# Decode attention with a feed-forward branch: keys one item ahead of values, the feed-forward input product as moving rows in mid-stream, output weights used earlier

## The chip, the cores and the metric

The kernel runs on one core of one Trainium2 chip. The metric is the time of one execution on the device in microseconds (us), as the median of several runs. The core has a matrix engine (TensorE, PE in the profile; its loads of the stationary operand are PEld), a vector engine (VectorE, DVE), an activation engine (ScalarE, ACT), a general engine (GpSimd, POOL) and a queue engine that issues transfers (SyncE, SP). Sixteen DMA engines move the data from memory into the core's on-chip buffer.

## The reference

One token per sequence (two sequences, `B = 2`) is decoded through two branches, and a gate mixes them:

```python
# x: (2, 1, 640); k_cache, v_cache: (2, 32, 4096, 128); wq: (640, 4096); wo: (4096, 640)
# w1: (640, 1728); w2: (1728, 640); all float32
g = sigmoid((x * gate_w).sum(-1, keepdims=True))
q = (x @ wq) split in 32 heads of 128
p = softmax(einsum("bhqd,bhkd->bhqk", q, k_cache) * 128 ** -0.5)
a = einsum("bhqk,bhkd->bhqd", p, v_cache) joined over heads @ wo
b = silu(x @ w1) @ w2
out = g * a + (1 - g) * b
```

Nearly all bytes are the two caches: 2 x 32 heads x 4096 positions x 128 numbers, once for keys and once for values, 268 MB together. Every byte is used once.

## The kernel before, in words

**Items.** The work is cut into 32 items, one for each pair of heads and sequence (`items`, L57). An item has one slab of keys and one of values, each 128 partitions x 8192 numbers (4 MB). Partition p holds 64 consecutive positions of one of the two heads.

**What is done with an item.** `mul` multiplies the keys in place by the query, which stands in every partition: columns from 44 of 64 on in GpSimd (L271), the others in two pieces on VectorE (L275). `scores` sums over the head dimension on VectorE (L281) and takes a maximum per partition (L284). `peak` turns these maxima on TensorE (`mt`, L288) and VectorE takes the maximum of each head (`mx`, L290). `weights` spreads it (`mb`, L296, `nb`, L298) and takes the exponentials on ScalarE (`pz`, L301). `total` adds the sums (`tot`, L312). `values` multiplies the weights with the values on TensorE, 16 products of 512 columns that go in turn to four groups of 32 output partitions (`pv`, L325). `combine` copies (`osb`, L336) and adds these groups (`po`, L339). `invert` (`rinv`, L317) and `scale` (`oT`, L348) divide, apply the gate and store the item's column for the output product.

**The loop.** In iteration i of the loop at L385 the program issues, in this order: the first piece of `mul` of item i, `peak` and `weights` of item i-1, the second piece of `mul` and `scores` of item i, and then `total`, `values`, `combine`, `invert` and `scale` of item i-1. Each engine takes its instructions in the order in which they are written (`manual_schedule`, L53).

**Slabs and the stream.** All large transfers go through five slabs (`SLOTS = 5`, L43). The list `stream` (L62 to L71) gives their order: query weights `wq` (first of three parts), input weights `w1`, then keys and values of each item in turn, the other parts of `wq` and the first part of the output weights `wo` after items 7, 13 and 18, and at the end `wo` part 1, `w2` and `wo` part 2. `pump` (L102) issues them on SP in this order; the transfer at place m of the list takes the slab of the one at place m-5 and so waits, on SP, until that one has been used up (`spend`). SP waits at the head of its queue, so a transfer that waits holds back all behind it. The last 64 rows of `w2` have a small tile of their own (`w2t`, L406).

**Before the loop.** `gates` makes the gate, `query_rows(0, ...)` (L237) multiplies x with the first part of `wq`, with x as the stationary operand and the weights as moving rows, `query(0)` (L253) spreads the query of the first head pair, and `ffn_in` (L195 to L214) makes the hidden vector of the feed-forward branch: for each of 14 groups of hidden units, five products with a 128-column piece of `w1` as the stationary operand and the two columns of x as moving data (`ph`, L202), then the SiLU and the gate on ScalarE and VectorE (L209 to L213).

**Output products.** `project(grp)` (L352) rearranges the results of two head pairs (`pp`, L356), copies them (`oP`, L365) and adds their product with four rows of weights to the bank `acc` (L184). Groups 0 to 2 are done in iteration 14, groups 3 to 5 behind the loop, then `ffn_out` (hidden vector times `w2`), groups 6 and 7 and the product with `w2t`. A copy (`ot`, L413) and two transfers end the program.

Of the kernel before, what the change touches and what calls it, by code (L numbers as in the profile page):

```python
# [8 lines left out]
F32 = mybir.dt.float32  # L9
# [6 lines left out]
def tile_gated_decode(  # L16
# [42 lines left out]
    QCH = ((0, 6), (6, 12), (12, HP))  # L59
    WOG = ((0, 3), (3, 6), (6, 8))  # L60

    stream = [("wq", 0), ("w1", 0)]  # L62
    for i in range(N):
        stream += [("k", i), ("v", i)]
        if i == 7:
            stream.append(("wq", 1))
        if i == 13:
            stream.append(("wo", 0))
        if i == 18:
            stream.append(("wq", 2))  # L70
    stream += [("wo", 1), ("w2", 0), ("wo", 2)]  # L71
    T = {}
    spent = set()
    nxt = [0]
# [106 lines left out]
    def accumulate(lhsT, w):  # L181
        m = lhsT.shape[1]
        for n in range(G):
            nc.tensor.matmul(  # L184
                acc[32 * n : 32 * n + m, :],
                lhsT,
                w[:, n * W : (n + 1) * W],
                start=(done[0] == 0),
                stop=(done[0] == NMM - 1),
            )  # L190
        done[0] += 1

    def ffn_in():  # L195
        w = T["w1", 0].rearrange("p (j f) -> p j f", j=J)
        ph = ps_s.tile([P, 512], F32, tag="sm", name="ph")
        for n in range(FR + 1):
            m = P if n < FR else FT
            for j in range(J):  # L200
                cols = w[:, j, n:FM:FR] if n < FR else w[:, j, FM:F]
                nc.tensor.matmul(  # L202
                    ph[:m, n * B : (n + 1) * B], cols, xs[:, :, j], start=(j == 0), stop=(j == J - 1)
                )
        for n0, n1, m in ((0, FR, P), (FR, FR + 1, FT)):
            k = n1 - n0
            src = ph[:m, n0 * B : n1 * B].rearrange("p (n b) -> p n b", b=B)
            e = const.tile([P, k, B], F32, name=f"he{n0}")[:m]
            nc.scalar.activation(e, src, AF.Exp, scale=-1.0)  # L209
            nc.vector.tensor_scalar_add(e, e, 1.0)  # L210
# [3 lines left out]
        spend("w1", 0)  # L214

    def ffn_out():
        w = T["w2", 0]
# [124 lines left out]
    def scale(i):  # L342
        hp, b = items[i]
        grp = hp // 2
        if grp not in O:
            O[grp] = const.tile([P, 4, B], F32, name=f"oT{grp}")
        h = 2 * (hp % 2)
        nc.vector.scalar_tensor_tensor(  # L348
            O[grp][:, h : h + 2, b], PO[i][:, :2], g[:, b : b + 1], R[i], op0=ALU.mult, op1=ALU.mult
        )  # L350

    def project(grp):  # L352
        pp = ps_s.tile([P, 512], F32, tag="sm", name="pp")
        for n in range(4):
            for h in range(4):
                nc.tensor.matmul(  # L356
                    pp[32 * h : 32 * h + 32, n * B : (n + 1) * B],
                    ident[:, n : P : 4],
                    O[grp][:, h, :],
                    start=True,  # L360
                    stop=True,
                )
        first = done[0] == 0
        oP = o_first if first else work.tile([P, 4, B], F32, name="oP")
        nc.scalar.copy(oP[:, :, :B], pp[:, : 4 * B].rearrange("p (n b) -> p n b", b=B))  # L365
# [12 lines left out]
    late = {  # L380
        8: [lambda: query_rows(1, 0), lambda: query_rows(1, 1)],
        14: [lambda: project(0), lambda: project(1), lambda: project(2)],
        19: [lambda: query_rows(2, 0), lambda: query_rows(2, 1)],
    }
    for i in range(N + 1):  # L385
        if i < N:
            mul(i, 0)
        if i >= 1:
            peak(i - 1)
            weights(i - 1)  # L390
        if i < N:
            mul(i, 1)
            scores(i)
            if i + 1 < N and items[i + 1][1] == 0:
                query(items[i + 1][0])
        if i >= 1:
            total(i - 1)
# [8 lines left out]
    nc.sync.dma_start(w2t, w2[FM:, :])  # L406
# [32 lines left out]
```

## Time and profile before

| | |
|---|---|
| median of 3 runs | 721.2 us (720.84 to 721.53) |
| the profiled execution's own time | 720.26 us |
| its span, first to last instruction | 718.5 us |
| bytes moved | 298.64 MB, mean 416 GB/s |
| busy: VectorE, TensorE, GpSimd, ScalarE | 501.2, 372.0, 181.8, 63.4 us |
| mean granted clock of TensorE | 0.659 |

The profile is of one execution. Its times count from the start of the span; the execution's own time is 1.76 us longer than its span. The page cuts the span in 40 slices of 18 us and gives for each the busy tenths of every engine, the granted clock of TensorE and what the DMA engines moved. The views by stretches give the same for stretches that one chooses. The chain of waits follows the work that ended last back from the end. For a transfer the profile gives the time from its issue on SP to its landing. A product in 32-bit numbers shows as two records on TensorE, so 16 products are 32 records.

### The profile page before, as it was taken

The numbers are of one execution on the slowest core, as the hardware profiler recorded it, in microseconds if no ns is written. First come the engines' busy times: TensorE is split into PE (matmuls) and PEld (weight loads), VectorE is DVE, ScalarE is ACT, GpSimd is POOL, SyncE is SP. The second block draws the span as 40 slices with busy tenths as digits, with TensorE's granted clock in tenths as the row PEclk, the third lists the DMA queues.
The fourth block names the chain that finished last, engine by engine and source line by source line (L and its number), as shares of the span: only waits on it lengthen the run. The fifth ranks groups of instructions, "written<-read, shape, count | busy, mean of one in ns | idle before, by whom it ended". The sixth has DMA issues, their size and how long they took to land.

```text
span 718.5 us, 5865 instructions
## 1 busy us (share of the span) xinstructions
PE 372.0 (52%) x2474; PEld 189.5 (26%) x2474; DVE 501.2 (70%) x247; ACT 63.4 (9%) x225; POOL 181.8 (25%) x44
## 2 busy tenths in 40 slices
PE   3992556454508455450845543544455545443476
PEld 1792222222203122220412221221122222221135
DVE  1006999878837777883777885777778887777740
ACT  0000011010100101010010100100010101000010
POOL 1023332123332222332222233332222333333300
PEclk9755576656658655665765565756665666666679
DMA  9999599999999999999999999999999999999993
GB/s 354 432 438 409 236 409 437 427 431 426 416 442 437 427 431 429 434 417 441 431 430 431 431 421 432 430 434 424 433 434 431 432 425 433 434 431 429 422 429 153
DMA packets 13162, 298.64 MB, mean 416 GB/s; under 512 B 1672, under 2 KB 1680, under 8 KB 3664
## 3 DMA queue, kind: packets, MB, share of 16 engines
q1 hardware_dynamic: 12712, 298.26, 97.1%
q8 instruction: 19, 0.31, 0.2%
q10 hardware_dynamic: 424, 0.01, 0.0%
q14 instruction: 7, 0.06, 0.0%
HBM read 298.26 MB, written 0.01 MB: 415 GB/s over the span
## 4 chain that ended last, share of the span: by engine, by line
DMA 53%; DVE 25%; PE 19%; ACT 1%; issue 1%; SPq 0%; DVEq 0%; ACTq 0%
DMA k<-in_A_k_cache_dram 50%; DVE k L275 12%; DVE s L281 12%; PE pv L325 8%; PE ph L202 5%; DMA w<-in_B_w_dram 3%; PE acc L184 2%; PE mb L296 1%; PE q L253 1%; PE tot L312 1%; ACT pz L301 1%; PE pp L356 1%; DVE mx L290 1%; PE po L339 0%; DVE he L210 0%
## 5 line engine op out<-in xcount | busy, mean ns | idle before, releaser
L271 POOL TENSOR_TENSOR k<-k,qsb 128x2560 f32<-128x2560 f32 x32 | 179.8, 5618 | 497.4 <-DMA k<-in_A_k_cache_dram 419.5
L275 DVE TENSOR_TENSOR k<-k,q 128x3072 f32<-128x3072 f32 x64 | 196.8, 3076 | 125.5 <-DMA k<-in_A_k_cache_dram 125.5
L281 DVE TENSOR_REDUCE s<-k 128x64 f32<-128x8192 f32 x32 | 278.0, 8686 | 3.7
L325 PE MATMUL pv<-v,pz 128*32 128x512 f32 x1024 | 183.5, 881 | 0.0
L296 PE MATMUL mb<-mx,nsc 1*128 1x1 f32 x128 | 31.4, 345 | 217.8 <-DVE mx L290 217.8
L296 PEld LDWEIGHTS mb<-mx,nsc 1*128 1x128 f32 x128 | 28.7, 309 | 230.1 <-DVE mx L290 224.8
L325 PEld LDWEIGHTS pv<-v,pz 128*32 128x32 f32 x1024 | 40.4, 153 | 113.1 <-issue 112.6
L288 PE MATMUL mt<-ident,m 128*1 128x128 f32 x64 | 15.0, 325 | 65.3 <-DVE m L284 65.3
L339 PE MATMUL po<-sel,osb 128*128 128x2 f32 x256 | 33.7, 254 | 22.9 <-ACT osb L336 22.9
L339 PEld LDWEIGHTS po<-sel,osb 128*128 128x128 f32 x256 | 31.0, 191 | 53.4 <-ACT osb L336 53.4
L298 ACT COPY nb<-mb 128x1 f32<-128x1 f32 x32 | 5.1, 160 | 359.5 <-PE mb L296 359.5
L336 ACT COPY osb<-pv 128x512 f32<-128x512 f32 x32 | 18.8, 586 | 196.5 <-PE pv L325 196.5
L202 PE MATMUL ph<-xs,w 128*128 128x2 f32 (+1 forms) x140 | 34.6, 385 | 1.3 <-DMA w<-in_B_w_dram 1.3
L202 PEld LDWEIGHTS ph<-xs,w 128*128 128x128 f32 (+1 forms) x140 | 34.5, 347 | 1.5 <-DMA w<-in_B_w_dram 1.5
L210 DVE TENSOR_SCALAR he<-he 128x26 f32<-128x26 f32 (+1 forms) x2 | 1.3, 636 | 47.7 <-ACT he L209 47.7
L312 PE MATMUL tot<-rs,ones 128*128 128x2 f32 x64 | 18.4, 357 | 21.1 <-ACT pz L301 20.9
L312 PEld LDWEIGHTS tot<-rs,ones 128*128 128x128 f32 x64 | 15.6, 304 | 26.8 <-ACT pz L301 26.8
L301 ACT ACTIVATE pz<-s,nb 64x64 f32<-64x64 f32 x64 | 22.1, 345 | 1.4
L288 PEld LDWEIGHTS mt<-ident,m 128*1 128x1 f32 x64 | 3.0, 81 | 68.7 <-DVE m L284 49.3
L237 PE MATMUL qr<-wq,xz 128*32 128x512 f32 (+1 forms) x100 | 19.4, 543 | 3.3 <-DMA wq<-in_A_wq_dram 3.3
L253 PE MATMUL q<-qrow,spread 64*128 64x128 f32 x64 | 18.0, 428 | 0.0
L348 DVE SCALAR_TENSOR_TENSOR oT<-po,g,rinv 128x2 f32<-128x2 f32 x32 | 7.0, 219 | 9.9 <-PE po L339 6.7
(49 smaller groups left out, 112.5 us busy)
## 6 DMA issues: line engine op xcount, KB each, us to landing
k<-in_A_k_cache_dram SPq DMA_DIRECT2D x32, 4096.0 KB, 27.2
v<-in_A_v_cache_dram SPq DMA_DIRECT2D x32, 4096.0 KB, 33.4
wo<-in_A_wo_dram SPq DMA_DIRECT2D x8, 1280.0 KB, 22.9
wq<-in_A_wq_dram SPq DMA_DIRECT2D x2, 3840.0 KB, 27.1
w<-in_B_w_dram SPq DMA_DIRECT2D x1, 4320.0 KB, 22.4
w<-in_B_w_dram SPq DMA_DIRECT2D x1, 4160.0 KB, 32.7
wq<-in_A_wq_dram SPq DMA_DIRECT2D x1, 2560.0 KB, 22.7
w2t<-in_B_w_dram SPq DMA_DIRECT2D x1, 160.0 KB, 22.1
```

Of the source, the lines that this page charges most:

```text
L202: nc.tensor.matmul(ph[:m, n * B : (n + 1) * B], cols, xs[:, :, j], start=(j == 0), stop=(j == J - 1))
L237: nc.tensor.matmul(ps[32 * hh : 32 * hh + 32, : (e - s) * DH], xz[:, j, :], w[:, j, s:e, hh, :], start=(j == 0), stop=(j == J - 1),)
L253: nc.tensor.matmul(qps[hp][:, b, :], spread[:, b, :], qrow[n][:, c : c + DH], start=True, stop=True)
L271: nc.gpsimd.tensor_mul(k[:, CV:, :], k[:, CV:, :], qsb[hp][:, b, None, :].to_broadcast([P, C - CV, DH]))
L275: nc.vector.tensor_mul(k[:, c0:c1, :], k[:, c0:c1, :], qps[hp][:, b, None, :].to_broadcast([P, c1 - c0, DH]))
L281: nc.vector.reduce_sum(S[i], kview(i), axis=AX.X)
L296: nc.tensor.matmul(mb[:, :1], nsc[:, hh, :], M[i][:, hh : hh + 1], start=(hh == 0), stop=(hh == 1))
L301: nc.scalar.activation(pz[i % NPZ][lo:hi, :, 4 * hh : 4 * hh + 4], S[i][lo:hi].rearrange("p (g c) -> p g c", c=4), AF.Exp, bias=nb[lo:hi], ...
L312: nc.tensor.matmul(t[:, :2], ones, rs2[i % NPZ], start=True, stop=True)
L325: nc.tensor.matmul(PV[i][32 * q : 32 * q + 32, :], pz[i % NPZ][:, gr, :], v[:, gr, :], start=(gr < 4), stop=(gr >= NG - 4),)
L336: nc.scalar.copy(osb.rearrange("p c d -> p (c d)"), PV[i])
L339: nc.tensor.matmul(po[:, :2], osb[:, c, :], sel[:, c : 8 : 4], start=(c == 0), stop=(c == 3))
```

## The change

- **Order of the stream.** Behind `wq` comes the first key slab. From there the keys of item i+1 stand ahead of the values of item i. `w1` stands behind the values of item 2, the other parts of `wq` and the first part of `wo` behind those of items 8, 12 and 19, and `wo` part 1 behind those of item 25. The end of the list is `w2` and `wo` part 2.
- **Feed-forward input product.** `ffn_in` now takes x (padded to 32 columns, `xz`) as the stationary operand and `w1` as moving rows: 4 column quarters of 416 into four groups of 32 output partitions, five products each, and five of 64 columns for the rest. ScalarE copies the rows (`hrow`), and 53 small products against the identity turn them into the same `ph` as before. It is called in iteration 3, and its SiLU (`ffn_act`) in iteration 4.
- **Output products.** `project` is split in `permute` (`pp`, `oP`) and the product itself. Groups 0 to 2 are done in iteration 13, groups 3 to 5 in iteration 26. Behind the loop both remaining groups are permuted first, then come `ffn_out` and the two products. `oP` has three buffers.
- `query(0)` now comes between the two parts of `query_rows(0, ...)`.

The core of the diff:

```diff
+    extra = {2: ("w1", 0), 8: ("wq", 1), 12: ("wo", 0), 19: ("wq", 2), 25: ("wo", 1)}
-    stream = [("wq", 0), ("w1", 0)]
+    stream = [("wq", 0), ("k", 0)]
     for i in range(N):
-        stream += [("k", i), ("v", i)]
...
-    stream += [("wo", 1), ("w2", 0), ("wo", 2)]
+        if i + 1 < N:
+            stream.append(("k", i + 1))
+        stream.append(("v", i))
+        if i in extra:
+            stream.append(extra[i])
+    stream += [("w2", 0), ("wo", 2)]
...
+    QF = FM // 4
+
     def ffn_in():
         w = T["w1", 0].rearrange("p (j f) -> p j f", j=J)
+        rows = ps_s.tile([P, 512], F32, tag="sm", name="hr")
+        for j in range(J):
+            for c in range(4):
+                nc.tensor.matmul(
+                    rows[32 * c : 32 * c + 32, :QF],
+                    xz[:, j, :],
+                    w[:, j, c * QF : (c + 1) * QF],
+                    start=(j == 0),
+                    stop=(j == J - 1),
+                )
+        hrow = const.tile([P, QF + FT], F32, name="hrow")
+        nc.scalar.copy(hrow[:, :QF], rows[:, :QF])
+        tail = ps_s.tile([P, 512], F32, tag="sm", name="hr")
+        for j in range(J):
+            nc.tensor.matmul(
+                tail[:32, :FT], xz[:, j, :], w[:, j, FM:F], start=(j == 0), stop=(j == J - 1)
+            )
+        nc.scalar.copy(hrow[:32, QF:], tail[:32, :FT])
+        spend("w1", 0)
         ph = ps_s.tile([P, 512], F32, tag="sm", name="ph")
-        for n in range(FR + 1):
-            m = P if n < FR else FT
-            for j in range(J):
-                cols = w[:, j, n:FM:FR] if n < FR else w[:, j, FM:F]
+        for n in range(FR):
+            for c in range(4):
+                q = slice(32 * c, 32 * c + 32)
                 nc.tensor.matmul(
-                    ph[:m, n * B : (n + 1) * B], cols, xs[:, :, j], start=(j == 0), stop=(j == J - 1)
+                    ph[q, n * B : (n + 1) * B],
+                    hrow[q, n:QF:FR],
+                    ident[q, 32 * c : 32 * c + B],
+                    start=True,
+                    stop=True,
                 )
...
+    def ffn_act(ph):
         for n0, n1, m in ((0, FR, P), (FR, FR + 1, FT)):
...
-    def project(grp):
+    OP = {}
+
+    def permute(grp):
         pp = ps_s.tile([P, 512], F32, tag="sm", name="pp")
...
+    def projects(groups):
+        for grp in groups:
+            permute(grp)
+        for grp in groups:
+            project(grp)
...
     query_rows(0, 0)
+    query(0)
     query_rows(0, 1)
-    query(0)
-    ffn_in()
     late = {
-        8: [lambda: query_rows(1, 0), lambda: query_rows(1, 1)],
-        14: [lambda: project(0), lambda: project(1), lambda: project(2)],
-        19: [lambda: query_rows(2, 0), lambda: query_rows(2, 1)],
+        3: [lambda: PH.append(ffn_in())],
+        9: [lambda: query_rows(1, 0), lambda: query_rows(1, 1)],
+        13: [lambda: projects(range(*WOG[0]))],
+        20: [lambda: query_rows(2, 0), lambda: query_rows(2, 1)],
+        26: [lambda: projects(range(*WOG[1]))],
     }
...
+        if i == 4:
+            ffn_act(PH[0])
         for f in late.get(i, []):
             f()
-    for grp in range(3, 6):
-        project(grp)
     nc.sync.dma_start(w2t, w2[FM:, :])
+    permute(6)
+    permute(7)
     ffn_out()
```

Three places show how the rows stand on an engine before and now. In them a name's number tells one buffer of a name from another; line numbers are those of the kernel that the rows are from.

SP at the start of the program, before (each row is one transfer, in the order of issue; the five that need no other's slab come first):

```order
L86 DMA wq_82<-in_A_wq_dram 128x5x1536
L91 DMA w1_84<-in_B_w1_dram 128x8640
L80 DMA k_86<-in_A_k_cache_dram 128x8192
L80 DMA v_88<-in_A_v_cache_dram 128x8192
L80 DMA k_90<-in_A_k_cache_dram 128x8192
L80 DMA v_166<-in_A_v_cache_dram 128x8192
L80 DMA k_256<-in_A_k_cache_dram 128x8192
L80 DMA v_263<-in_A_v_cache_dram 128x8192
```

and now:

```order
L85 DMA wq_82<-in_A_wq_dram 128x5x1536
L79 DMA k_84<-in_A_k_cache_dram 128x8192
L79 DMA k_86<-in_A_k_cache_dram 128x8192
L79 DMA v_88<-in_A_v_cache_dram 128x8192
L79 DMA k_90<-in_A_k_cache_dram 128x8192
L79 DMA v_171<-in_A_v_cache_dram 128x8192
L79 DMA k_178<-in_A_k_cache_dram 128x8192
L79 DMA v_198<-in_A_v_cache_dram 128x8192
L90 DMA w1_226<-in_B_w1_dram 128x8640
L79 DMA k_255<-in_A_k_cache_dram 128x8192
```

`w1` moved from the second place to the ninth, and of the first five transfers three are keys instead of two. The sixth waits for the slab of the first in both, the seventh for that of the second: `w1` before, the first keys now.

TensorE, before, where the feed-forward input product stood (ahead of the first `mt`):

```order
L237 MATMUL qr_154<-wq_82,xz_120 32x256 x10
L253 MATMUL q_168<-qrow_141,spread_105 128x128 x2
L202 MATMUL ph_173<-xs_78,w1_84 128x2 x65
L202 MATMUL ph_173<-xs_78,w1_84 64x2 x5
L288 MATMUL mt_269<-ident_92,m_265 1x128
```

and now, in iteration 3 (`pv_317` is the product with the values of item 2, `mt_434` belongs to item 3):

```order
L353 MATMUL pv_317<-v_198,pz0_110 32x512 x16
L367 MATMUL po_338<-sel_103,osb_336 128x2 x4
L201 MATMUL hr_346<-w1_226,xz_120 32x416 x20
L212 MATMUL hr_369<-w1_226,xz_120 32x64 x5
L221 MATMUL ph_378<-ident_92,hrow_367 32x2 x52
L228 MATMUL ph_378<-ident_92,hrow_367 64x2
L316 MATMUL mt_434<-ident_92,m_308 1x128
```

70 products with weights as stationary operand became 25 with weights as moving rows and 53 small ones, and they stand behind the products of item 2.

TensorE behind the last values, before (`pv_2095` is item 31):

```order
L325 MATMUL pv_2095<-v_1966,pz1_114 32x512 x16
L339 MATMUL po_2114<-sel_103,osb_2112 128x2 x4
L356 MATMUL pp_2122<-oT3_996,ident_92 32x2 x16
L184 MATMUL acc_127<-wo_2016,oP_2139 2x160 x16
...
L184 MATMUL acc_127<-w2_2020,hT_126 2x160 x52
L356 MATMUL pp_2280<-oT6_1762,ident_92 32x2 x16
L184 MATMUL acc_127<-wo_2069,oP_2297 2x160 x16
L356 MATMUL pp_2315<-oT7_1977,ident_92 32x2 x16
L184 MATMUL acc_127<-wo_2069,oP_2332 2x160 x16
L184 MATMUL acc_127<-w2t_122,hT_126 2x160 x4
```

and now:

```order
L353 MATMUL pv_2213<-v_2088,pz1_114 32x512 x16
L367 MATMUL po_2232<-sel_103,osb_2230 128x2 x4
L386 MATMUL pp_2241<-oT6_1777,ident_92 32x2 x16
L386 MATMUL pp_2260<-oT7_2099,ident_92 32x2 x16
L183 MATMUL acc_127<-w2_2117,hT_126 2x160 x52
L183 MATMUL acc_127<-wo_2140,oP_2258 2x160 x16
L183 MATMUL acc_127<-wo_2140,oP_2277 2x160 x16
L183 MATMUL acc_127<-w2t_122,hT_126 2x160 x4
```

Groups 3 to 5 (oT3 to oT5) left this place, and both remaining `pp` stand ahead of the product with `w2`.

More of the change, by code (lines that the diff above doesn't have):

```diff
@@ L60, in tile_gated_decode @@
     WOG = ((0, 3), (3, 6), (6, 8))
-    stream = [("wq", 0), ("w1", 0)]
+    extra = {2: ("w1", 0), 8: ("wq", 1), 12: ("wo", 0), 19: ("wq", 2), 25: ("wo", 1)}
+    stream = [("wq", 0), ("k", 0)]
     for i in range(N):
-        stream += [("k", i), ("v", i)]
[L65 to L70, printed above, removed]
-    stream += [("wo", 1), ("w2", 0), ("wo", 2)]
+        if i + 1 < N:
[4 more added lines that the diff above has]
+    stream += [("w2", 0), ("wo", 2)]
     T = {}
@@ L191, in accumulate @@
         done[0] += 1
+    QF = FM // 4
     def ffn_in():
         w = T["w1", 0].rearrange("p (j f) -> p j f", j=J)
+        rows = ps_s.tile([P, 512], F32, tag="sm", name="hr")
[17 more added lines that the diff above has]
+        spend("w1", 0)
         ph = ps_s.tile([P, 512], F32, tag="sm", name="ph")
-        for n in range(FR + 1):
-            m = P if n < FR else FT
-            for j in range(J):
-                cols = w[:, j, n:FM:FR] if n < FR else w[:, j, FM:F]
+        for n in range(FR):
+            for c in range(4):
+                q = slice(32 * c, 32 * c + 32)
                 nc.tensor.matmul(
-                    ph[:m, n * B : (n + 1) * B], cols, xs[:, :, j], start=(j == 0), stop=(j == J - 1)
-                )
+                    ph[q, n * B : (n + 1) * B],
[3 more added lines that the diff above has]
+                    stop=True,
+                )
+        nc.tensor.matmul(
+            ph[:FT, FR * B : (FR + 1) * B], hrow[:32, QF:], ident[:32, :B], start=True, stop=True
+        )
+        return ph
+    def ffn_act(ph):
         for n0, n1, m in ((0, FR, P), (FR, FR + 1, FT)):
@@ L213, in ffn_in @@
             nc.vector.tensor_mul(hT[:m, n0:n1, :], src, e)
-        spend("w1", 0)
     def ffn_out():
@@ L362, in project @@
                 )
-        first = done[0] == 0
-        oP = o_first if first else work.tile([P, 4, B], F32, name="oP")
-        nc.scalar.copy(oP[:, :, :B], pp[:, : 4 * B].rearrange("p (n b) -> p n b", b=B))
+        OP[grp] = o_first if grp == 0 else work.tile([P, 4, B], F32, name="oP", bufs=3)
+        nc.scalar.copy(OP[grp][:, :, :B], pp[:, : 4 * B].rearrange("p (n b) -> p n b", b=B))
+    def project(grp):
         n0 = next(k for k, (a, z) in enumerate(WOG) if a <= grp < z)
@@ L368, in project @@
         for n in range(4):
-            accumulate(oP[:, n, :] if done[0] == 0 else oP[:, n, :B], w[:, n * D : (n + 1) * D])
+            accumulate(OP[grp][:, n, :] if done[0] == 0 else OP[grp][:, n, :B], w[:, n * D : (n + 1) * D])
         if grp == WOG[n0][1] - 1:
             spend("wo", n0)
+    def projects(groups):
[3 more added lines that the diff above has]
+            project(grp)
     gates()
     query_rows(0, 0)
+    query(0)
     query_rows(0, 1)
-    query(0)
-    ffn_in()
     late = {
-        8: [lambda: query_rows(1, 0), lambda: query_rows(1, 1)],
-        14: [lambda: project(0), lambda: project(1), lambda: project(2)],
-        19: [lambda: query_rows(2, 0), lambda: query_rows(2, 1)],
+        3: [lambda: PH.append(ffn_in())],
[3 more added lines that the diff above has]
+        26: [lambda: projects(range(*WOG[1]))],
     }
+    PH = []
     for i in range(N + 1):
```

## The prediction

> **What bounds the kernel now.** I read the page's head and slices first. For DMA each digit is the busy tenth of a slice of 18 us, and the next row what was moved in it.
>
> ```profile
> span 718.5 us, 5865 instructions
> DMA  9999599999999999999999999999999999999993
> GB/s 354 432 438 409 236 409 437 427 431 426 416 442 437 427 431 429 434 417 441 431 430 431 431 421 432 430 434 424 433 434 431 432 425 433 434 431 429 422 429 153
> DMA packets 13162, 298.64 MB, mean 416 GB/s; under 512 B 1672, under 2 KB 1680, under 8 KB 3664
> ```
>
> No compute engine is full (VectorE 70%), but the DMA engines are, in all slices except the fifth and the last. So the transfers set the end, and I look for the time in which they don't flow. The view by stretches (its last three columns are granted clock, DMA share, GB/s) gives:
>
> ```profile
> 24.00:60.00 36.00, 34.56 (x140) 34.46 (x140) 1.14 (x2) 0.19 (x1) 11.20 (x2) 0.55 1.01 436
> 60.00:135.00 75.00, 36.76 (x192) 15.94 (x192) 73.52 (x36) 6.81 (x26) 16.87 (x3) 0.60 0.89 374
> 135.00:690.00 555.00, 268.61 (x1614) 120.25 (x1610) 422.13 (x193) 51.20 (x182) 151.69 (x27) 0.65 1.00 430
> ```
>
> From 135 us on the stream is full at 430 GB/s: nothing that the change does to keys, values or engines there can gain. Two losses are left: the hole between 60 and 135 us, and what comes behind the last transfer. The timeline of SP shows where the hole is from (start, duration, transfer issued):
>
> ```profile
> 1.49 0.61 SPq L91 DMA_DIRECT2D w<-in_B_w_dram  x1
> 3.36 0.46 SPq L80 DMA_DIRECT2D k<-in_A_k_cache_dram  x1
> 22.05 0.33 SPq L80 DMA_DIRECT2D v<-in_A_v_cache_dram  x1
> 58.59 0.33 SPq L80 DMA_DIRECT2D k<-in_A_k_cache_dram  x1
> 76.56 0.33 SPq L80 DMA_DIRECT2D v<-in_A_v_cache_dram  x1
> 89.55 0.33 SPq L80 DMA_DIRECT2D k<-in_A_k_cache_dram  x1
> ```
>
> Five transfers are out by 3.8 us, the sixth follows at 22, the seventh only at 58.6 us, when the slab of `w1` is free, the eighth at 76.6. The chain of waits says who held that slab (start, duration, what):
>
> ```profile
> 1.49 22.41 DMA w<-in_B_w_dram
> 23.95 34.63 PE ph L202 x140
> ...
> 58.82 1.12 DVE he L210
> ...
> 61.76 6.00 DVE k L275 x2
> 67.85 8.70 DVE s L281
> ```
>
> ```profile
> 34.95 5.61 POOL L271 TENSOR_TENSOR k<-k,qsb 128x2560 f32<-128x2560 f32 x1 [32.33 <-DMA k<-in_A_k_cache_dram]
> w<-in_B_w_dram SPq DMA_DIRECT2D x1, 4320.0 KB, 22.4
> ```
>
> TensorE works 34.6 us on the feed-forward input product (its 4320 KB of weights came first), and VectorE starts the first keys at 61.7 us although GpSimd had them at 35. The queue of transfers runs dry meanwhile.
>
> **The change part by part.**
>
> *1. The early hole.* At 430 GB/s the bytes of the stretch 60 to 135 us would take 75 x 374 / 430 = 65.2 us, so the hole is worth 9.8 us. By the DMA share (0.89) it is 75 x 0.11 = 8.25 us. The bytes are what must be moved, so I take 9.8 and keep 8.25 as the lower end. From 24 to 60 us the stream ran at 436 with VectorE idle; it will now run beside VectorE, as it does later at 430, which costs 36 x 6 / 436 = 0.5 us. Term: 9.3 us, if no other hole opens.
>
> Does one open? A slab of 4096 KB takes 4.194 MB / 430 GB/s = 9.75 us. `wq`, then one transfer of 4320 KB, landed at 1.49 + 22.41 = 23.9 us; in its place the first keys (4096 KB) land at about 23.4. From there, every 9.75 us: keys 1 at 33, values 0 at 43, keys 2 at 53, values 1 at 62, keys 3 at 72, values 2 at 82, `w1` at 92, keys 4 at 102. VectorE's work for an item is this:
>
> ```profile
> PE 372.0 (52%) x2474; PEld 189.5 (26%) x2474; DVE 501.2 (70%) x247; ACT 63.4 (9%) x225; POOL 181.8 (25%) x44
> L271 POOL TENSOR_TENSOR k<-k,qsb 128x2560 f32<-128x2560 f32 x32 | 179.8, 5618 | 497.4 <-DMA k<-in_A_k_cache_dram 419.5
> L275 DVE TENSOR_TENSOR k<-k,q 128x3072 f32<-128x3072 f32 x64 | 196.8, 3076 | 125.5 <-DMA k<-in_A_k_cache_dram 125.5
> L281 DVE TENSOR_REDUCE s<-k 128x64 f32<-128x8192 f32 x32 | 278.0, 8686 | 3.7
> ```
>
> At most 501.2 / 32 = 15.7 us an item (GpSimd's 5.6 us run beside it), against 19.5 us of stream. So VectorE does items 0, 1 and 2 from 23.4 to 39, 55 and 70 us, and waits for keys 3: it has caught up. The slabs come free in time: keys 2's fellow, the seventh transfer (keys 3), waits for keys 0, used by 39, and is due on the queue by 62; values 2 wait for keys 1, 55 against 72; keys 4 wait for keys 2, 70 against 92. The least margin is about 17 us. Behind that each pair has the same five slabs as before, with values used about 9 us behind their landing instead of waiting for the next keys.
>
> *2. The feed-forward product in mid-stream.* Removed are 34.6 us of TensorE. Added in iteration 3: 20 products of 416 columns in four groups, like `pv` (16 of 512 columns in 5.16 us, row below), so 5.16 x 20 x 416 / (16 x 512) = 5.2 us; five of 64 columns, under 1 us; two copies on ScalarE, under 0.8; 53 small products like `pp` (16 in 0.60 us, row below), 2.0 us. Together about 9 us, with 34.6 as the upper bound, if moving rows save nothing. TensorE waits there for `w1` (92 us), and behind it stand `mt` and `mb` of item 3, for which VectorE waits in front of the second piece of keys 4. At 9 us TensorE is free at 101, before keys 4 land at 102: nothing is late. At 34.6 us it would be free at 127, VectorE would end keys 4 at about 140, and the transfer that takes their slab (values 5) is due at 139: a hole of 2 us at most. I take 0. The SiLU on VectorE (61.76 - 58.8 = 3 us) makes item 4 cost 18.7 of 19.5 us and is covered; uncovered it costs 3.
>
> *3. `query(0)` ahead, `wo` and `wq` later by one item, w1's place on SP.* All are hidden by the full stream, with margins as in part 1; every transfer passes the one SP queue in list order as before. Bytes are the same. 0.
>
> *4. The end.* These are the last rows of the timeline, the chain of the last item, and the landing of the last transfers (KB, us from issue to landing):
>
> ```profile
> 687.75 0.53 SPq L406 DMA_DIRECT2D w2t<-in_B_w_dram  x1
> 690.13 0.28 DVE L290 TENSOR_REDUCE mx<-mt 1x2 f32<-1x128 f32 x1 [0.28 <-PE mt L288]
> 693.15 5.17 PE L325 MATMUL pv<-v,pz 128*32 128x512 f32 x32
> 699.04 1.05 PE L339 MATMUL po<-sel,osb 128*128 128x2 f32 x8 [0.71 <-ACT osb L336]
> 707.90 2.40 PEld L184 LDWEIGHTS acc<-w,hT 128*2 128x2 f32 x73 [0.93 <-issue]
> 712.60 0.60 PE L356 MATMUL pp<-oT,ident 128*32 128x2 f32 x32
> 713.55 1.27 PE L184 MATMUL acc<-wo,oP 128*2 128x160 f32 x32 [0.34 <-ACT oP L365]
> 714.75 0.45 PE L184 MATMUL acc<-w2t,hT 64*2 64x160 f32 x8
> 715.26 0.33 DVE L413 COPY ot<-acc 128x160 f32<-128x160 f32 x1 [14.91 <-PE acc L184]
> w2t<-in_B_w_dram SPq DMA_DIRECT2D x1, 160.0 KB, 22.1
> v<-in_A_v_cache_dram SPq DMA_DIRECT2D x32, 4096.0 KB, 33.4
> ```
>
> `w2t` landed at 687.75 + 22.1 = 709.85 us, but the copy `ot` starts at 715.26: 5.4 us of products still stand behind it. What was on the way there, groups 3 to 5 and two `pp`, is now done earlier. Behind the last keys now come values 30 and 31 (8192 KB), `w2` (4160), `wo` (2560) and `w2t` (160): 15.4 MB, 35.9 us. Work from there: 15.7 us of VectorE, 10 us from `mx` (690.13) to the end of `po` (700.09), 1 us of `pp` and copy: 26.7 us. `w2` lands 29.4 us behind the last keys, so that chain is hidden by 2.7 us; if it is longer by more than that, the excess counts in full. `ffn_out` (104 records, 4.1 us at the pace of 1.27 us for 32) ends 2.4 us before the last landing, group 6 runs when its weights come (3 us before), and behind the last landing stand group 7 and `w2t`: 1.27 + 0.45 = 1.7 us. Gain 5.4 - 1.7 = 3.7. Best case: group 7's weights land early enough to be done, gain 5.0. Worst: all of it runs at a low clock. The granted clock was 0.50 in a stretch and 1.00 in another:
>
> ```profile
> 76.00:80.00 4.00, 0.59 (x2) 0.11 (x2) 3.97 (x4) 0.00 (x0) 0.00 (x0) 0.50 0.78 262
> 700.00:705.00 5.00, 4.09 (x165) 3.38 (x169) 0.22 (x1) 0.50 (x3) 0.00 (x0) 1.00 0.94 395
> 351.38 2.26 PE L184 MATMUL acc<-wo,o_first 128*32 128x160 f32 x32 [0.29 <-ACT o_first L365]
> ```
>
> 32 records of `acc` took 2.26 us at 351 us and 1.27 at the end, a factor of 1.78. At the slow pace `ffn_out` takes 7.3 us and ends 0.4 behind the last landing, groups 6 and 7 take 2.26 each, `w2t` 0.8: 5.7 us behind it, a loss of 0.3 to before.
>
> The Trainium skill speaks against the fast pace here: "TensorE: Matmul & The Clock Gate", section "Part 1: The HAM clock gate", says that an idle window of about 3.4 us halves the clock and a busy one restores it. The trace agrees in part: TensorE idle until 76 us, clock 0.50; but with 34.6 of 36 us busy on two-column products the clock was 0.55, so products of two columns did not count as busy. By that rule the pauses between the last landings would bring the slow pace, and the sum would be rival A's.
>
> *Sum.* Span 718.5 - 9.3 - 3.7 = 705.5 us; the execution's own time 720.26 - 13.0 = 707.3. The profiled execution lies 0.94 us under the median of the runs shown, so against that median: 721.2 - 13.0 = **708.2 us**. Extremes of the terms: 8.25 - 0.5 - 0.3 = 7.5 us of gain (713.7), and 9.8 + 5.0 = 14.8 (706.4).
>
> **The rivals.**
>
> *A, slow clock at the end.* Between the last landings TensorE pauses, `ffn_out` and both groups run at 0.50: 4.0 us more, 712.2. For it: the mean clock is 0.65 or less in all long stretches. Against: from 700 to 705 us it is 1.00, though TensorE had paused for copies before. This is also the outcome by the rule of the Trainium skill told in part 4.
>
> *B, the early hole closes by half.* SP's queue holds back all behind a waiting head, and part 1's margins are reckoned. With a hole of 4.9 us left: 713.1. Against: margins of 17 us.
>
> *C, the stream gets faster.* With keys ahead slabs are free sooner and more transfers wait at the engines. If the 555 us ran at the 436 of the early stretch, it would be 555 x 6 / 436 = 7.6 us: 700.6. Against: the share is 1.00 already at 430.
>
> *D, the hole only moves.* `w1` blocks TensorE in mid-stream at its bound and delays more than I see; only the end gains: 717.5.
>
> *E, slower: the keys wait for the values.* On VectorE `oT` of item i stands ahead of the keys of item i+2, and needs `po`, so the values, which now land behind the keys of i+1. Values i+2 are issued when keys i+1 are used up, and keys i+4 are multiplied only behind their `oT`: a loop over three items. With 39 us from issue to landing (four slabs queued), 7.6 from there to `oT` (5.17 + 0.6 + 1.05 and handing over) and 15.7 it takes 62.3 us, 20.8 an item, 1.3 too many: 31 x 1.3 = 40 us, less the 13 gained: 748. Against: the 33 or 39 us are waiting behind other slabs, so then the stream is full. It decides only if a landing with an empty queue took over 58.5 - 23.3 = 35 us, and one slab takes 9.75.
>
> **How the numbers follow.** As summed 0.70; A 0.12; B 0.06; C 0.05; D 0.02; E 0.03; nothing at all 0.02. Less than 0.2% (1.4 us) can't be told from no change here. Faster: all but E and the last, 0.95; same 0.02; slower 0.03. The range 705.0 to 713.0 holds the sum with its bounds and A, and leaves out C to E and the half of B.
>
> **What would show it.** Right: a first `k` product on VectorE near 23 us; no slice under 400 GB/s but the first and the last; the seventh transfer issued near 39 us; `ph` gone from the chain; under 2.5 us from the landing of `w2t` to `ot`. Wrong: a slice under 400 in the first ten (part 1, B, D); clock 0.5 and `acc` at 2.26 us behind the last landing (A); 135 to 690 us at another rate than 430 (C); VectorE's waits on `po` in place of those on keys (E).

## The result, and the profile after

The changed kernel takes 708.08 us (median, 707.82 to 708.37) against 721.02 us before (four runs; the 721.2 ahead of the prediction was the median of three of them): a ratio of 0.9822 with a 95% interval of 0.9805 to 0.9839, 12.9 us less. The prediction said 708.2. Its profiled execution takes 707.82 us and has a span of 706.0 us.

The page's head and slices of the changed kernel (busy tenths of the DMA engines and GB/s in 40 slices):

```profile
span 706.0 us, 5888 instructions
DMA  8999999999999999999999999999999999999995
GB/s 342 444 424 436 427 435 428 433 426 433 429 420 440 428 433 429 421 440 428 433 429 430 431 431 430 429 430 430 433 428 434 422 434 434 424 438 426 437 424 217
```

The slice of 236 GB/s is gone; between the first and the last slice none is under 420. The stretches say the same (last columns: clock, DMA share, GB/s):

```profile
24.00:60.00 36.00, 13.26 (x70) 6.12 (x66) 35.61 (x14) 3.06 (x12) 16.82 (x3) 0.63 0.99 427
60.00:135.00 75.00, 39.00 (x314) 18.30 (x318) 54.00 (x31) 6.91 (x26) 16.80 (x3) 0.64 1.01 433
135.00:680.00 545.00, 271.42 (x1772) 121.97 (x1764) 410.68 (x183) 49.09 (x177) 146.04 (x26) 0.66 1.00 430
```

From 60 to 135 us the stream runs at 433 instead of 374 GB/s. VectorE (third pair of numbers) now works 35.6 of the 36 us from 24 to 60, where before it worked 1.1. Behind that the rate is the 430 of before.

The timeline of SP shows what became of the late transfers (start, duration, transfer):

```profile
25.18 0.33 SPq L79 DMA_DIRECT2D v<-in_A_v_cache_dram  x1
38.85 0.33 SPq L79 DMA_DIRECT2D k<-in_A_k_cache_dram  x1
54.07 0.33 SPq L79 DMA_DIRECT2D v<-in_A_v_cache_dram  x1
54.51 0.38 SPq L90 DMA_DIRECT2D w<-in_B_w_dram  x1
69.70 0.33 SPq L79 DMA_DIRECT2D k<-in_A_k_cache_dram  x1
```

The seventh transfer goes out at 38.85 us, not at 58.59, the eighth at 54.07, not at 76.56. In the kernel before, the seventh waited for the slab of `w1` and the eighth for that of the first keys; now it is the seventh that waits for the first keys, and they are used up at 38.85 us instead of 76.56.

Which of the two waits opened the hole is read from the kernel before, in its stretches (last number: GB/s) and on VectorE:

```profile
62.00:70.00 8.00, 0.00 (x0) 0.00 (x0) 7.90 (x3) 0.00 (x0) 0.00 (x0) 0.50 0.98 422
70.00:71.00 1.00, 0.00 (x0) 0.00 (x0) 1.00 (x1) 0.00 (x0) 0.00 (x0) 0.50 1.22 524
71.00:72.00 1.00, 0.00 (x0) 0.00 (x0) 1.00 (x1) 0.00 (x0) 0.00 (x0) 0.50 0.01 0
...
58.82 1.11 DVE L210 TENSOR_SCALAR he<-he 128x26 f32<-128x26 f32 x1 [47.49 <-ACT he L209]
61.68 3.33 DVE L275 TENSOR_TENSOR k<-k,q 128x3072 f32<-128x3072 f32 x1
```

The stream is full until 71 us, 12 us after the wait for the slab of `w1` is over, so that wait alone cost nothing. It runs dry at 71, when the seven transfers issued so far have been moved, and flows again when the eighth goes out at 76.56. That one waits for the scores of the first keys. These keys had landed by 34.95 us, when GpSimd began them, but on VectorE the SiLU stands ahead of them and waits for the old product, so VectorE began them only at 61.68. The ninth transfer (89.55 us) comes late for the same reason: it waits for the first values, which are used behind these scores, and the stream is dry again from 88 to 90 us. The old product opened the hole by holding VectorE, not by holding the slab of `w1`.

The end of the timeline, with the issue of the last transfer:

```profile
661.18 0.52 SPq L445 DMA_DIRECT2D w2t<-in_B_w_dram  x1
...
694.20 6.06 PE L183 MATMUL acc<-w,hT 128*2 128x160 f32 x104 [1.30 <-DMA w<-in_B_w_dram]
700.09 2.35 PE L183 MATMUL acc<-wo,oP 128*2 128x160 f32 x64
702.37 0.45 PE L183 MATMUL acc<-w2t,hT 64*2 64x160 f32 x8
702.89 0.33 DVE L454 COPY ot<-acc 128x160 f32<-128x160 f32 x1 [10.80 <-PE acc L183]
```

and, from the table of transfers, its landing (KB, us from issue):

```profile
w2t<-in_B_w_dram SPq DMA_DIRECT2D x1, 160.0 KB, 39.8
```

The last transfer lands at 661.18 + 39.8 = 701.0 us, 8.9 us earlier than before (709.85), and the copy `ot` starts 1.9 us behind it instead of 5.4. So 8.9 us come from the hole and 3.5 from the end, together 12.4 of the 12.5 us of the span.

### The profile page after: what moved, and what is told of

Same layout as the page of the kernel before. It is cut to its first block, busy times and chain, and to the rows that moved or that the text cites. A ratio compares the mean times of both kernels' runs of the same rounds, so it can differ in the third digit from the quotient of the medians.

```text
span 706.0 us, 5888 instructions
## 1 busy us (share of the span) xinstructions
PE 353.6 (50%) x2490; PEld 161.7 (23%) x2490; DVE 505.2 (72%) x247; ACT 64.0 (9%) x227; POOL 181.7 (26%) x44
## 4 chain that ended last, share of the span: by engine, by line
DMA 69%; DVE 25%; PE 5%; issue 0%; SPq 0%; ACT 0%; DVEq 0%
DMA k<-in_A_k_cache_dram 42%; DMA v<-in_A_v_cache_dram 22%; DVE s L309 14%; DVE k L303 9%; DMA w<-in_B_w_dram 5%; PE pv L353 4%; PE acc L183 1%; DVE he L241 1%; DVE mx L318 0%; DVE m L312 0%; PE po L367 0%; SPq L85 0%; ACT osb L364 0%; DVE rinv L345 0%; DVE he L240 0%
## 5 line engine op out<-in xcount | busy, mean ns | idle before, releaser
L353 PE MATMUL pv<-v,pz 128*32 128x512 f32 x1024 | 186.0, 893 | 94.7 <-DMA v<-in_A_v_cache_dram 94.7
L376 DVE SCALAR_TENSOR_TENSOR oT<-po,g,rinv 128x2 f32<-128x2 f32 x32 | 7.0, 220 | 60.6 <-PE po L367 60.3
L265 PE MATMUL qr<-wq,xz 128*32 128x512 f32 (+1 forms) x100 | 22.4, 606 | 5.6 <-DMA wq<-in_A_wq_dram 5.6
L316 PE MATMUL mt<-ident,m 128*1 128x128 f32 x64 | 12.8, 282 | 16.5 <-DVE m L312 16.5
L281 PEld LDWEIGHTS q<-qrow,spread 64*128 64x128 f32 x64 | 14.4, 312 | 1.8 <-ACT qrow L272 1.6
L329 ACT ACTIVATION_READ_ACCUMULATOR pz<-s,nb 64x1 f32 x64 | 11.8, 185 | 0.0
L265 PEld LDWEIGHTS qr<-wq,xz 128*32 128x32 f32 x100 | 6.4, 124 | 19.1 <-issue 15.2
L183 PE MATMUL acc<-wo,oP 128*2 128x160 f32 x224 | 9.8, 337 | 0.0
## 6 DMA issues: line engine op xcount, KB each, us to landing
k<-in_A_k_cache_dram SPq DMA_DIRECT2D x32, 4096.0 KB, 41.2
w2t<-in_B_w_dram SPq DMA_DIRECT2D x1, 160.0 KB, 39.8
```

What stands on the lines that cost most here:

```text
L183: nc.tensor.matmul(acc[32 * n : 32 * n + m, :], lhsT, w[:, n * W : (n + 1) * W], start=(done[0] == 0), stop=(done[0] == NMM - 1),)
L265: nc.tensor.matmul(ps[32 * hh : 32 * hh + 32, : (e - s) * DH], xz[:, j, :], w[:, j, s:e, hh, :], start=(j == 0), stop=(j == J - 1),)
L281: nc.tensor.matmul(qps[hp][:, b, :], spread[:, b, :], qrow[n][:, c : c + DH], start=True, stop=True)
L329: nc.scalar.activation(pz[i % NPZ][lo:hi, :, 4 * hh : 4 * hh + 4], S[i][lo:hi].rearrange("p (g c) -> p g c", c=4), AF.Exp, bias=nb[lo:hi], ...
L353: nc.tensor.matmul(PV[i][32 * q : 32 * q + 32, :], pz[i % NPZ][:, gr, :], v[:, gr, :], start=(gr < 4), stop=(gr >= NG - 4),)
```

## The experiments

A table first. "Last landing" is the issue of `w2t` plus its time to landing; "behind" is the start of `ot` less that; both are from the profile of each kernel, the time is its median.

| kernel | time, us | last landing | behind |
|---|---|---|---|
| before | 721.0 | 709.85 | 5.4 |
| changed | 708.08 | 701.0 | 1.9 |
| moving rows at the start only | 712.87 | 700.95 | 6.9 |
| keys ahead only | 720.24 | 711.1 | 4.0 |
| both of these | 709.59 | 701.2 | 3.5 |
| changed, old product in mid-stream | 709.31 | 702.2 | 1.7 |
| changed, values behind their own keys | 712.99 | 701.6 | 8.0 |
| changed, middle output weights last | 707.87 | 701.1 | 1.9 |

### Moving rows at the start only

```diff
     query(0)
-    ffn_in()
+    ffn_act(ffn_in())
```

> The kernel before, with the feed-forward input product as moving rows but still ahead of the loop, and with w1 still second in the stream. Nothing else is changed. Theory of the held slab: the hole from 60 to 135 us came from the 34.6 us for which the old form held the slab of w1; the new form (6.2 + 0.7 + 2.2 us in the changed kernel) frees it near 31 us and VectorE starts near 36 us, so the hole closes whole, 9 us gain, and the end stays as before (5.4 us of products behind the last landing): 711 to 713 us. Rival, keys ahead and the order of the stream are what matters: within 2 us of before, 719 to 721.

712.87 us, a ratio of 0.9877 (0.9853 to 0.9901) to before. From the timeline of this kernel:

```profile
23.91 3.70 PE L202 MATMUL hr<-w,xz 128*32 128x416 f32 x40
28.18 0.33 SPq L80 DMA_DIRECT2D k<-in_A_k_cache_dram  x1
30.61 0.18 DVE L240 TENSOR_SCALAR he<-he 128x26 f32<-128x26 f32 x1 [19.19 <-ACT he L239]
35.01 6.08 DVE L304 TENSOR_TENSOR k<-k,q 128x3072 f32<-128x3072 f32 x2 [2.40 <-DMA k<-in_A_k_cache_dram]
...
692.18 2.31 PE L184 MATMUL acc<-wo,oP 128*2 128x160 f32 x32 [0.29 <-ACT oP L394]
```

and from its stretches:

```profile
60.00:135.00 75.00, 34.66 (x193) 14.81 (x192) 59.10 (x27) 6.35 (x23) 19.64 (x5) 0.66 1.00 430
```

The slab of `w1` is free at 28.2 us, VectorE begins the first keys at 35.0 us, as they land, and the stream runs at 430 GB/s from 60 to 135 us. The last landing is as early as in the changed kernel (700.95). So the faster form alone closes the hole. This run frees the slab and VectorE at once; that VectorE is what counts is read from the kernel before (above). At the end it loses 1.5 us more than before: behind the last values TensorE has the same products in the same order, but the granted clock was 0.51 from 692 to 694 us, and 32 records of `acc` took 2.31 us instead of 1.27 at 1.00.

### Keys ahead only

```diff
-    stream = [("wq", 0), ("w1", 0)]
+    stream = [("wq", 0), ("w1", 0), ("k", 0)]
     for i in range(N):
-        stream += [("k", i), ("v", i)]
+        if i + 1 < N:
+            stream.append(("k", i + 1))
+        stream.append(("v", i))
```

> The kernel before, with the keys of item i+1 ahead of the values of item i in the stream, and nothing else: w1 stays second, the old product stays ahead of the loop, wo part 1 stays at the end. Theory of the held slab: the hole stays (VectorE still starts at 62 us; the seventh transfer still waits for w1, keys 3 wait for keys 0 until 77 us, values 2 for keys 1 until 92), and only the end gains about 3 us, since 9.75 us more of transfers now follow the last keys: 716 to 720 us. Rival, the gain is the deeper queue that keys ahead give: 712 us or less.

720.24 us, a ratio of 0.9984 (0.9975 to 0.9994): 0.24 us above the range, on the side of the theory. The stretch of the hole in this kernel:

```profile
60.00:135.00 75.00, 36.20 (x192) 15.85 (x192) 73.70 (x33) 7.15 (x27) 17.84 (x4) 0.63 0.86 364
```

At 364 GB/s the hole is worth 75 x 66 / 430 = 11.5 us, more than the 9.8 of before; the end gives back 1.4 (4.0 behind the landing instead of 5.4). The first keys are used up at 75.7 us here, as late as before. Keys ahead do not close the hole.

### Both of these, nothing else

```diff
+    stream = [("wq", 0), ("w1", 0), ("k", 0)]
...
+        if i + 1 < N:
+            stream.append(("k", i + 1))
+        stream.append(("v", i))
...
+    ffn_act(ffn_in())
```

> The kernel before with two edits only: the feed-forward input product as moving rows, still ahead of the loop with w1 second in the stream, and the keys one item ahead of the values. w1 and the middle output weights stay where they were. If the two edits add up: the hole closes (9 us), and the products at the end stand 4 us behind the last landing as with keys ahead alone, instead of 5.4: 709.5 to 711 us. If the place of w1 in mid-stream matters for itself: 712 or more.

709.59 us, a ratio of 0.9842 (0.9826 to 0.9859). It is in the expected range, but the two edits do more than add up: together they gain 11.5 us, alone 8.5 and 1.1. The landing is at 701.2 us; the 2 us more come at the end, 3.5 us behind the landing against 6.9 with the moving rows only. The place of `w1` in mid-stream, the halves of `project` and the earlier output weights together are worth the 1.5 us to the changed kernel, nearly all at the end (3.5 behind the landing against 1.9).

### The old product in mid-stream

```diff
     def ffn_in():
-        rows = ps_s.tile([P, 512], F32, tag="sm", name="hr")
...
+        for n in range(FR + 1):
+            m = P if n < FR else FT
+            for j in range(J):
+                cols = w[:, j, n:FM:FR] if n < FR else w[:, j, FM:F]
+                nc.tensor.matmul(
+                    ph[:m, n * B : (n + 1) * B], cols, xs[:, :, j], start=(j == 0), stop=(j == J - 1)
+                )
```

> The changed kernel with the old form of the feed-forward input product (70 products with the weights as stationary operand, 34.6 us) in iteration 3. Theory of part 2 of the prediction: TensorE is held from 92 to 127 us, the slab of w1 is due for keys 6 at about 129 and that of keys 4 for values 5 at 139, so a hole of at most 2 us opens: 708 to 710 us. Rival D, the blocked TensorE delays more than that reckoning sees: 5 us or more, 713 to 718.

709.31 us (0.9843, 0.9822 to 0.9865), in the theory's range. From its timeline:

```profile
128.39 0.28 DVE L292 TENSOR_REDUCE mx<-mt 1x2 f32<-1x128 f32 x1 [21.76 <-PE mt L290]
```

and from its stretches:

```profile
135.00:150.00 15.00, 8.24 (x48) 4.23 (x44) 14.32 (x16) 2.25 (x9) 1.11 (x1) 0.61 0.90 370
```

VectorE waits 21.8 us for a blocked TensorE, and the stream loses 15 x 60 / 430 = 2.1 us just where it was reckoned, near 139 us. Here too the loss comes by way of VectorE. So with the first keys ahead of `w1` even 34.6 us of TensorE nearly vanish: the form of the product and its place are two ways to close the same hole, not two gains.

### Values behind their own keys

```diff
-    stream = [("wq", 0), ("k", 0)]
+    stream = [("wq", 0)]
     for i in range(N):
-        if i + 1 < N:
-            stream.append(("k", i + 1))
-        stream.append(("v", i))
+        stream += [("k", i), ("v", i)]
```

> The changed kernel with the values of each item straight behind its own keys again, the rest as changed. Theory: no hole opens at the start either (keys 1 land at 43 us, VectorE is never late), so what keys ahead are worth shows at the end alone: behind the last keys stand 11.2 MB, 26 us, but the work of the last item takes 27 us and then come the product with w2 and two groups (6 to 8 us), so the products end 8 to 10 us behind the last landing instead of 1.9: 713 to 716 us. Rival, keys ahead do nothing: 707.5 to 709. Rival of the deeper queue: the hole comes back, 718 or more.

712.99 us (0.9891, 0.9873 to 0.9909). No hole (431 GB/s from 60 to 135 us), the landing at 701.6, but the products end far behind it. The end of its timeline:

```profile
689.76 0.22 DVE L310 TENSOR_REDUCE m<-s 128x1 f32<-128x64 f32 x1
693.18 5.99 PE L351 MATMUL pv<-v,pz 128*32 128x512 f32 x32
701.85 5.13 PE L181 MATMUL acc<-w,hT 128*2 128x160 f32 x104
709.60 0.33 DVE L452 COPY ot<-acc 128x160 f32<-128x160 f32 x1 [8.40 <-PE acc L181]
```

The product with `w2` starts when the last item is through, at 701.85 us, when all transfers have landed; in the changed kernel it starts at 694.20, when `w2` lands. This is what keys ahead are worth: 4.9 us by the medians, nearly all at the end, because the last keys arrive 9.75 us earlier in the stream. (The profiled execution, 714.59 us, is the slowest of the four: of its 6.8 us of longer span, 6.1 stand behind the last landing.)

### The middle output weights last

```diff
-    extra = {..., 19: ("wq", 2), 25: ("wo", 1)}
-    stream += [("w2", 0), ("wo", 2)]
+    extra = {..., 19: ("wq", 2)}
+    stream += [("wo", 1), ("w2", 0), ("wo", 2)]
...
-        26: [lambda: projects(range(*WOG[1]))],
+    projects(range(*WOG[1]))
     nc.sync.dma_start(w2t, w2[FM:, :])
```

> The changed kernel with wo part 1 back at the end of the stream (ahead of w2) and groups 3 to 5 behind the loop, the rest as changed. Theory: with keys ahead this part of the change is worth nothing, for 3.9 MB more follow the last keys (9.1 us) and hide the 6 us of the three groups; the products still end 2 to 3 us behind the last landing: 707.5 to 709 us. Rival, the use in mid-stream took those 6 us off the end: 712 to 715.

707.87 us (0.9825, 0.9811 to 0.9838), the changed kernel's time. The end of its timeline:

```profile
682.81 4.61 PE L183 MATMUL acc<-wo,oP 128*2 128x160 f32 x96
694.59 5.80 PE L183 MATMUL acc<-w,hT 128*2 128x160 f32 x104 [5.07 <-DMA w<-in_B_w_dram]
```

The three groups run while TensorE waits for `w2` anyway, and 5.1 us of waiting are left. Using these weights in mid-stream is worth nothing here. So what made the changed kernel 1.5 us shorter than the run with both edits is the place of `w1`, the permutations ahead of the product with `w2` or one of the smaller moves; no run separates these.

### Fewer slabs

The edit with four slabs; the other has three.

```diff
-    SLOTS = 5
+    SLOTS = 4
```

> The changed kernel with four slabs instead of five. By the margins of the prediction (least 17 us with five slabs, one slab is 9.75 us of stream) 7 us are left, so no hole opens and the stream stays full: 707.5 to 709.5 us. Rival, a deeper queue is what keeps the rate at 430 GB/s: slower by 0.5% or more, 712 and up.

> The changed kernel with three slabs. By the same reckoning the margin is gone at the start (values 1 wait for keys 1 until 54.5 us, but the queue is empty from 51 on: about 5 us of hole) and about 2 us later on: 711 to 718 us, the loss in the first 80 us. Rival, margins reckoned so are too wide by more than 2 us: every item then loses the excess, 730 us or more.

With four slabs 708.0 us (0.9826, 0.9812 to 0.984), no change: a margin of at least one slab, 9.75 us, was there. With three 721.36 us (1.0015, 0.9999 to 1.0031), above the expected 711 to 718 and under the rival's 730. The stretches of the kernel with three slabs:

```profile
24.00:60.00 36.00, 12.58 (x64) 5.97 (x60) 35.61 (x14) 3.39 (x13) 16.19 (x3) 0.62 0.91 384
135.00:680.00 545.00, 262.95 (x1734) 119.04 (x1734) 394.57 (x180) 48.11 (x172) 141.27 (x26) 0.66 0.99 421
```

At the start 36 x 46 / 430 = 3.9 us are lost, about what was reckoned. But 545 x 9 / 430 = 11.4 us go in the rest, about 0.4 us an item, where a margin of 2 us was said to be left. So the reckoning is too kind by a good 2 us there. The shortest time from issue to landing in this kernel is 12.1 us, for a slab that takes 9.75 us of stream; that difference would explain it, but no run separated it.

### A busy TensorE at the end

```diff
+            if i == N:
+                warm(1)
             combine(i - 1)
...
     permute(7)
+    warm(3)
     ffn_out()
```

> The changed kernel with four added products of 512 columns at the end, one behind the last values and three behind the last permutation, whose results nobody reads; they only keep TensorE busy while it waits. In the changed kernel the product with w2 ran at a clock of 0.50 (104 records in 6.06 us) and the products ended 1.4 us later than the last landing allows. Theory of the slow clock (rival A): 104 records in 4.1 to 4.8 us, 0.5 to 1.4 us off the end, 706.7 to 707.6 us. If the clock does not follow such work, 6.06 us stay and the time is 708 to 708.5.

707.99 us (0.9825, 0.9812 to 0.9838), no gain. The end of its timeline:

```profile
695.15 3.56 PE L183 MATMUL acc<-w,hT 128*2 128x160 f32 x97
701.38 1.27 PE L183 MATMUL acc<-wo,oP 128*2 128x160 f32 x32 [1.45 <-DMA wo<-in_A_wo_dram]
703.09 0.33 DVE L465 COPY ot<-acc 128x160 f32<-128x160 f32 x1 [11.18 <-PE acc L183]
```

One of its stretches (third number from the end: the clock):

```profile
696.00:698.00 2.00, 2.00 (x66) 1.39 (x63) 0.00 (x0) 0.00 (x0) 0.00 (x0) 1.00 0.62 255
```

and the same one of the changed kernel:

```profile
696.00:698.00 2.00, 2.00 (x36) 1.14 (x32) 0.00 (x0) 0.00 (x0) 0.00 (x0) 0.50 0.61 247
```

The clock is 1.00 instead of 0.50, and the product with `w2` is done in 4.5 us (694.35 to 698.84) instead of 6.06. But then the last group waits 1.45 us for its weights, until 701.38. In the changed kernel the slow product ended just in time for them: the landing sets the end, and the slow clock costs next to nothing there (707.99 against 708.08 us). That the added products raised the clock is not shown: in the two kernels that follow it was 1.00 from 692 to 700 us as well, without them.

### Half of the scores

```diff
-        nc.vector.reduce_sum(S[i], kview(i), axis=AX.X)
+        nc.vector.reduce_sum(S[i], kview(i)[:, :, : DH // 2], axis=AX.X)
```

> The changed kernel with the sum of scores over half of the head dimension only (the other half of the product is left out, so the output is another): VectorE does 4.3 us less per item, 139 us less in all. Theory, the stream alone sets the end and VectorE stands 4 us per item clear of it: 707 to 708.5 us. Rival, VectorE's work is still on the path between the items: 705 or less.

707.84 us (0.9818, 0.9804 to 0.9833). The busy times of this kernel:

```profile
PE 350.1 (50%) x2490; PEld 161.4 (23%) x2490; DVE 363.8 (52%) x247; ACT 64.0 (9%) x227; POOL 181.7 (26%) x44
```

VectorE does 363.8 us instead of 505.2, and the time stays: the stream alone sets it.

### Keys first of all

```diff
-    stream = [("wq", 0), ("k", 0)]
+    stream = [("k", 0), ("wq", 0)]
```

> The changed kernel with the first keys ahead of the first part of wq in the stream. From 2 to 10 us the stream moved 335 GB/s with wq at its head, a loss of 8 x 95 / 430 = 1.8 us. If that is the shape of wq (rows of 6 KB), keys at the head gain up to 1.5 us: 706.5 to 707.5 us; VectorE starts at 33 us and 7 us of the least margin are left. If it is a start-up of any transfer, or wq is as slow behind the keys: 707.7 to 708.5.

707.33 us (706.92 to 707.68; 0.9811, 0.9796 to 0.9825), 0.75 us under the changed kernel and the fastest version of the study. The two spreads don't overlap, but the two kernels were measured on different occasions, and their ratios to before do overlap (0.9796 to 0.9825 here, 0.9805 to 0.9839 there): the gain is likely, not certain. The first stretches of this kernel:

```profile
0.00:2.00 2.00, 0.00 (x0) 0.00 (x0) 1.10 (x8) 0.23 (x1) 1.40 (x9) 1.00 0.72 197
2.00:10.00 8.00, 0.00 (x0) 0.00 (x0) 0.82 (x4) 1.05 (x1) 0.61 (x4) 1.00 0.95 398
10.00:24.00 14.00, 3.00 (x12) 2.43 (x14) 1.50 (x5) 0.17 (x1) 0.00 (x0) 1.00 0.99 401
```

and of the changed kernel:

```profile
0.00:2.00 2.00, 0.00 (x0) 0.00 (x0) 1.10 (x8) 0.26 (x1) 1.40 (x9) 1.00 0.03 1
2.00:10.00 8.00, 1.51 (x7) 1.51 (x8) 1.72 (x6) 1.02 (x1) 0.61 (x4) 1.00 0.96 335
10.00:24.00 14.00, 9.83 (x40) 3.66 (x42) 0.55 (x4) 1.12 (x3) 0.00 (x0) 1.00 1.05 450
```

With the keys at the head bytes flow already in the first 2 us (197 GB/s against 1), but behind them, with `wq` among the transfers, the stream is slower: 401 from 10 to 24 us, where 450 stood. Both readings were partly right. The bytes of the first 24 us are 9.19 MB against 8.98, a lead of 0.5 us of stream. The last landing is 0.4 us earlier (700.6), so of the 0.9 us between the two profiled spans about half is from the start; the rest stands at the end, where this execution had the clock of 1.00.

## Why the prediction was right

- **Part 1, the early hole.** Said 9.3 us; the last landing came 8.9 us earlier. The first `k` product on VectorE was said for 23.4 us and started at 23.95, the seventh transfer for 39 and went at 38.85. No other hole opened. The prediction pointed at two things, the late seventh transfer and the late start of VectorE; the second is the one that counted, since the stream ran dry only at 71 us, 12 us after the seventh transfer had gone out. Its margins rest on VectorE's times for the first keys, so the sum is not touched by this. The margins are shown to be at least 9.75 us by four slabs (no change); with three they turn out about 2 us too wide. The moving rows alone close the hole, and so, but for 2 us, does the mid-stream place with the old product (together with keys ahead, which alone don't). With 433 GB/s from 60 to 135 us in the changed kernel, and 1.2 us lost with the old product in mid-stream, rivals B and D fall. The reading that a deeper queue does it falls too: with keys ahead the keys' time from issue to landing went from 27.2 to 41.2 us (median) while the rate stayed at 430 GB/s. Rival C falls with that.
- **Part 2, the product in mid-stream.** Said about 9 us for the new form; it ran from 93.28 to 102.1 us. Its bound, the old form in that place, was said to cost 2 us at most near 139 us: 2.1 us were lost between 135 and 150, and 1.2 us in the time.
- **Part 2, the SiLU.** Wrong in size without effect: said 3 us on VectorE, it took 7.1 (121.4 to 128.5 us), of which 5.35 are one tiny product (last section). So it does not fit into the slack of one item, as the prediction had it: item 5 starts 5.7 us late on VectorE, and the slabs' margin covers it.
- **Part 3** is right as a whole, but it took the move of `wo` for hidden and part 4 then counted it as a cause of the shorter end. The run with these weights last shows that it is none: the 9.75 us of values that now follow the last keys hide the three groups wherever they are.
- **Part 4, the end.** Said 1.7 us behind the last landing, measured 1.9. Its gain of 3.7 was 3.5. The chain of the last item was said to be hidden by 2.7 us; TensorE waited 1.30 us for `w2`. The step in it that the trace contradicts is the pace of the product with `w2`: said 4.1 us, it took 6.06, mostly at a clock of 0.50, as rival A had it. Rival A's price of 4 us still fails, since the clock was back for the two groups (0.98 from 699 to 700 us, 64 records in 2.35 us) and the rest was covered by the wait for their weights. The slow pace itself was read from a row of another shape (`o_first`); the run with the moving rows at the start has it for the same shape, 2.31 us for 32 records. The prediction had set beside rival A the rule of the Trainium skill ("TensorE: Matmul & The Clock Gate", section "Part 1: The HAM clock gate") that an idle window of about 3.4 us halves the clock and a busy one restores it. The trace agrees with it in part: the clock was 0.50 until 699 us and back 4.8 us after the product with `w2` had begun, but it had fallen by 692.5 us, behind pauses of 0.7 us and products of two columns, with no pause of 3.4 us.
- **Rival E** falls: VectorE does wait for `po` (60.3 us in 29 waits, 2.1 us each), but inside the time in which it would wait for keys. Half of the scores left out changes nothing.

The sum was 13.0 us and the measured difference of the spans 12.5, of the medians 12.9. That the forecast comes within 0.1 us of the median is partly luck: the two terms were 0.4 and 0.2 us too large, and the forecast set the profiled execution 0.94 us under its median, where that of the changed kernel lay 0.26 under.

## What to carry to other kernels

When one queue of transfers is full nearly always, look for the stretches in which it isn't and ask whose slab the head of the queue waits for at that moment, and what keeps the engine that uses this slab up: here VectorE had the first keys in reach, but stood behind a slow product of TensorE in its own order, and either a faster form or a later place of that product was enough. A long wait of the queue's head costs nothing while earlier transfers still flow: the 34.6 us for the slab of `w1` were such a wait. Write for each slab when it is free and when its next transfer is due: the least margin told beforehand what four slabs and even the old product would cost, but leave a few us a transfer, as three slabs show. What the order of a full stream can still buy lies at its end: the last transfer should be one behind which little work is left, and work that is faster than its operands arrive is not worth speeding up.

## What the runs showed of the hardware that was not expected

A tiny VectorE product can stand for the whole of a GpSimd product. In the changed kernel's timeline:

```profile
121.96 0.19 DVE L241 TENSOR_TENSOR he<-he,gc 128x26 f32<-128x26 f32 x1
122.74 5.57 POOL L299 TENSOR_TENSOR k<-k,qsb 128x2560 f32<-128x2560 f32 x1 [13.79 <-DMA k<-in_A_k_cache_dram]
122.98 5.35 DVE L241 TENSOR_TENSOR he<-he,gc 64x2 f32<-64x2 f32 x1
```

The product of 128x26 took 0.19 us ahead of the GpSimd product; the smaller one of 64x2, started 0.24 us behind it, took 5.35 and ended with it. Both its inputs are in the on-chip buffer, as are GpSimd's, while VectorE's large `k` product reads the query from the accumulation banks and keeps its 3.3 us beside GpSimd. In the kernel with the middle output weights last and in that with the busy TensorE at the end it stood beside GpSimd's product too and took 5.44 and 5.57 us. In the kernel with four slabs the small product came before GpSimd's and took 0.15 us. The Trainium skill says so ("SBUF — State Buffer", section "Who interferes with whom": a VectorE instruction with two inputs from that buffer contends with a GpSimd instruction that reads it, and the later one blocks for the whole instruction), and these rows agree.

And the clock: while TensorE was busy without a pause on products of two columns, the granted clock was 0.50. The first row is from the kernel before, the second from the one with the old input product in mid-stream (which stands there until 128 us):

```profile
40.00:58.00 18.00, 18.00 (x75) 17.98 (x75) 0.00 (x0) 0.00 (x0) 4.25 (x2) 0.50 1.00 430
100.00:135.00 35.00, 33.46 (x143) 30.21 (x146) 9.86 (x4) 1.03 (x5) 11.24 (x2) 0.50 1.00 429
```
